# Decoding the weights of a dense layer beside earlier attention units, with four attention units done in split precision instead of plain fp32

## The chip, the cores and the metric

The kernel runs on one core of a Trainium2 chip. The metric is the time of one execution on the device, in microseconds (us). Three runs of the kernel before took 1157.36, 1158.56 and 1164.47 us; their median is 1158.56 us. The engines are named as in the profile: PE is TensorE (matrix products), DVE is VectorE, ACT is ScalarE, POOL is GpSimd, SP is SyncE, which here only issues transfers.

## The reference

Three layers follow one another on 3072 tokens (4 sequences of 768) of width 512. The first is attention with 8 heads of width 64, over a window of 128 positions and 4 sink positions. The second is a dense layer with weights of 512 x 2048 and 2048 x 512 that computes h - tanh(h) between its products. The third is a layer of 8 experts, each with weights of 512 x 1024 and 1024 x 512, of which every token goes through the one that its logits choose.

```python
scores = scale * np.matmul(q, k.transpose(0, 1, 3, 2))
keep = is_sink | in_window
a = softmax(np.where(keep, scores, -1e9))     # written out in the reference
x = np.matmul(a, v)                           # heads side by side: 3072 x 512
h = x @ w_in
x = (h - np.tanh(h)) @ w_out
e_idx = np.argmax(x @ w_gate + modality_bias[modality_id], axis=1)
out[mask] = gate_w[mask, None] * (np.maximum(x[mask] @ w1[e], 0.0) @ w2[e])
```

All of it is in fp32. The kernel reaches that precision in one of two ways: a product of plain fp32 operands, or a product of operands that are split into a high and a low part of type fp32r, of which two or three products are added up in PSUM. The weights w_in and w_out reach the core as 64-bit floats and are turned into 32-bit ones on it.

## The kernel before

**Attention units.** Queries are cut into 12 chunks of 256 tokens; a chunk and a head are a unit, 96 units U in all. `a_load` and `a_loadv` fetch q, k and v of a unit. `a_S` makes two score tiles s (128 queries each): PE computes them, DVE masks them (L317) and takes the row maximum while it copies them to e (L324), ACT exponentiates (L326). `a_norm` divides by the row sum, `a_T` transposes e on PE (L348, L349) into one PSUM tile T, and `a_PV` multiplies by v into the PSUM tile R. The first nf = 14 units are plain: scores are one fp32 product per tile (L315), `a_plain` copies T on ACT, and the product with v is four fp32 products (L406 to L410). All units from 14 on are pair units: `a_split` casts q to A (ACT) and k to K (DVE, L211), and subtracts to get the low parts B (POOL) and the lower half of K (DVE, L214); `a_splitv` does so with v (cast on ACT, subtraction on POOL); scores are two fp32r products (L312, L313); `a_pair` has two more subtractions on DVE (L386 for fl, L387 for sT); the product with v is up to seven fp32r products (L414 to L420), followed by an addition on DVE (L423 for xp). A plain unit's division by the row sum is on ACT (L336), a pair unit's on POOL (L338).

**The dense layer.** It has 16 pairs of weight tiles, f = 0 to 15: `w_load` fetches 128 x 512 64-bit numbers of w_in (rawi) and of w_out (rawo), 512 KB each. `w_decode` turns one such tile into fp32 with three instructions on DVE (L145, L147, L149, by way of a PSUM tile ypi or ypo that shares its two buffers with R), then casts to the high part on ACT (L209) and subtracts for the low part on POOL (L214). For each chunk c and each f, `L1` makes twelve products with w_in (L176) into h, `gact` computes the activation in steps that alternate between ACT and DVE (L187 to L192), `g_split` casts on ACT (L209) and subtracts on POOL (L214), and `L2` makes twelve products with w_out (L246) into acc. `xsplit` (L211 and L214 on xt) splits a chunk's attention output before its `L1`.

**The expert layer.** When eleven chunks are through, routing has sorted their tokens (`r_order`) into pages of 256 tokens of one expert each, and SP reads from the table `order` which expert and which token list each page has. For a page g and f = 0 to 7: `m_wload` fetches 512 KB of weights (mr), `m_wsplit` casts them on ACT (mh, L753) and subtracts on DVE (ml, L754); `m_list` fetches the token list (mpl) and turns it into indices on DVE (mi L764, ms L766), `m_xload` gathers the rows on POOL (mx, L777), `m_xT` transposes them, `m_L1` (L803), `m_L2` (L820) and `m_out` (L829) do the rest. Page 0 begins while the last chunk's dense layer still runs.

**What sets the order.** Every step is added to a list with a number that says when it is due: unit U at 2U - 15.64 plus an offset, `L1` of chunk c and tile f at 16c + f, a page's step at offsets from its own start. The list is sorted by that number and emitted; a scheduler that simulates the engines then decides, instruction by instruction, in which order each engine's queue stands. The numbers are fields of one dictionary in `__init__` (line 45): wl and wls (start and step of the weight loads), wd and wds (of the decodes), nf, and for the pages mwl and mws (how far ahead of its product a page weight is loaded and split). Loads and lists of the first pages are not placed before the number `first`, at which the order of eleven chunks is known. Decoded weights, raw weights and page weights come from one pool of 33 slots, of which 32 hold the decoded weights while the dense layer runs.

Of the kernel before, what the change touches and what calls it, by code (L numbers as in the profile page):

```python
# [40 lines left out]
class Kern:  # L41
    def __init__(self, tc, a):
        self.tc, self.nc, self.a = tc, tc.nc, a
        self.Wi, self.Wo = {}, {}
        self.o = dict(tc='a', xa='g', mt0=-0.28, gz='v', mxe=11, lx='v', nf=14, efh='a', trc=-14.17, tpf=-1.86, xhi='v', vhi='a', vlo='g', qhi='a', khi='v', sT='a', tr='a', ev='a', glo='g', whi='a', wlo='g', gk=0, wl=-8.54, wls=1.25, wd=-3.86, wds=1.05, wo=1, bs=2, be=3, bE=3, bV=1, bg=2, btr=1, bxt=1, pt={'h': 'h', 's': 'r', 'T': 'r', 'R': 'R', 'x': 'R', 'y': 'R'}, pb=(('r', 2), ('h', 2), ('R', 2)), tl=-9.97, ts=-5.86, tv=-4.34, tsv=-2.34, tS=-5.24, dS=0.07, tN=-4, dN=0.5, tT=-1.78, dT=0.35, tPV=-0.39, txs=-0.28, tg=0.64, tre=0.05, trl=0.48, trr=3.39, u0=-15.64, g=2, lag=3.4, raw=2, sp=2, ghi='a', qlo='g', klo='v', eh='v', xlo='v', x2=4, me=13, mxl=8.77, mxt=1.5, mlag=1.45, mwl=9.99, mws=3.27, mm=0, ev0='v', ghi0='a', vhi0='a', sT0='a', qhi0='a', xlo0='g', eh0='v', y=2)

    def e(self, k, start):
        return self.o.get(k + "0", self.o[k]) if start else self.o[k]
# [786 lines left out]
    def m_events(self, add, g, t, t0=-1e9, ts=(0, 1)):  # L835
        n8 = FF // P
        o = self.o
        at = lambda d, fn, *a: add(max(t + d, t0), fn, *a)
        at(-o["me"], self.m_expert, g)
        x0 = o["mxe"] if g == 1 else o["mxl"]  # L840
        if g < EARLY and t0 > 0:
            add(t0, self.m_list, g)
        else:
            at(-x0 - .01, self.m_list, g)
        at(-x0, self.m_xload, g, ts)
        for j in ts:
            at(-o["mxt"] + 0.5 * j, self.m_xT, g, j, ts)
            at(n8 + o["mlag"] - 0.5, self.m_out, g, j)
        for f in range(n8):
            at(f - o["mwl"], self.m_wload, g, f)  # L850
            at(f - o["mws"], self.m_wsplit, g, f)
            at(f, self.m_L1, g, f, ts)
            at(f + o["mlag"], self.m_L2, g, f, ts)

# [205 lines left out]
```

## Time and profile before

| | us |
|---|---|
| median of three runs | 1158.56 |
| profiled execution | 1158.06 |
| its span, from first to last instruction | 1156.3 |
| PE busy in the span | 1109.8 |
| DVE busy | 845.4 |
| ACT busy | 696.1 |
| POOL busy | 586.4 |

The profiled execution's time holds 1.8 us that lie outside the span. The mean clock granted to PE over the span was 0.989 of full speed. Busy times are averages over stages that have different limits: the plain units at the start, the decoding of the weights beside the first chunk, the eleven chunks after it, and the pages. Only what happens in the stage that the change touches says what it is worth. A row of the timeline gives the start in us, the length in us, engine, line, the tile written and the tiles read, how many instructions it groups, and in brackets the idle time before it with what ended it.

### The profile page before, as it was taken

The numbers are of one execution on the slowest core, as the hardware profiler recorded it, in microseconds if no ns is written. First come the engines' busy times: TensorE is split into PE (matmuls) and PEld (weight loads), VectorE is DVE, ScalarE is ACT, GpSimd is POOL, SyncE is SP. The second block draws the span as 40 slices with busy tenths as digits, with TensorE's granted clock in tenths as the row PEclk, the third lists the DMA queues.
The fourth block names the chain that finished last, engine by engine and source line by source line (L and its number), as shares of the span: only waits on it lengthen the run. The fifth ranks groups of instructions, "written<-read, shape, count | busy, mean of one in ns | idle before, by whom it ended". The sixth has DMA issues, their size and how long they took to land. (4 is left out here: it accounts for less than half of the span.)

```text
span 1156.3 us, 22180 instructions
## 1 busy us (share of the span) xinstructions
PE 1109.8 (96%) x7143; PEld 978.2 (85%) x7143; DVE 845.4 (73%) x2244; ACT 696.1 (60%) x1669; POOL 586.4 (51%) x847
## 2 busy tenths in 40 slices
PE   7999889999999999999999999999899999999995
PEld 3467678998999999998999998998788989999984
DVE  3389988787888878798888789765687566666640
ACT  3566656666667666667576666664746555555531
POOL 2257775667676767676676767662203211121111
PEclk9999999999999999999999999999999999999998
DMA  6356422223232322222131322100857776677600
GB/s 201 92 188 220 142 71 49 81 74 69 75 70 70 70 78 62 88 65 86 52 94 52 92 65 68 60 10 19 304 188 247 239 231 219 214 233 239 211 21 22
DMA packets 74957, 136.79 MB, mean 118 GB/s; under 512 B 16144, under 2 KB 51216, under 8 KB 74832
## 3 DMA queue, kind: packets, MB, share of 16 engines
q1 hardware_dynamic: 70064, 122.40, 35.0%
q0 software_dynamic: 4768, 12.87, 3.4%
q8 instruction: 59, 0.97, 0.4%
q14 instruction: 66, 0.54, 0.2%
HBM read 122.60 MB, written 12.91 MB: 117 GB/s over the span
## 5 line engine op out<-in xcount | busy, mean ns | idle before, releaser
L176 PE MATMUL h<-xt,wi 128*128 128x256 f32 x2304 | 349.7, 290 | 10.7 <-ACT wi L209 4.3
L176 PEld LDWEIGHTS h<-xt,wi 128*128 128x128 f32 x2304 | 313.5, 193 | 31.1 <-ACT wi L209 6.1
L246 PE MATMUL acc<-wo,g 128*128 128x512 f32 x1152 | 313.9, 399 | 6.0 <-ACT g L209 5.1
L246 PEld LDWEIGHTS acc<-wo,g 128*128 128x128 f32 x1152 | 201.9, 189 | 39.0 <-ACT g L209 5.7
L754 DVE TENSOR_TENSOR ml<-mr,mh 128x1024 fp32r<-128x1024 f32 x104 | 129.3, 1247 | 57.9 <-ACT mh L753 56.7
L214 POOL TENSOR_TENSOR g<-gy,g 128x512 fp32r<-128x512 f32 x96 | 130.9, 1364 | 74.0 <-ACT g L209 70.1
L803 PE MATMUL mh<-mxt,mh 128*128 128x256 f32 (+1 forms) x832 | 154.4, 282 | 1.0 <-ACT mxt L791 0.7
L803 PEld LDWEIGHTS mh<-mxt,mh 128*128 128x128 f32 x832 | 135.7, 191 | 9.5 <-ACT mxt L791 0.9
L820 PE MATMUL macc<-mh,mg 128*128 128x512 f32 x400 | 141.6, 399 | 0.2
L753 ACT CAST mh<-mr 128x1024 fp32r<-128x1024 f32 x104 | 108.9, 1051 | 44.5 <-PE macc L820 29.6
L356 POOL TENSOR_SCALAR_AFFINE_SELECT X<-fl 128x512 fp32r<-128x512 f32 (+1 forms) x192 | 113.2, 612 | 41.8 <-DVE fl L386 23.5
L829 POOL DMA_INDIRECT out_dram<-mo,mi x25 | 26.2, 1046 | 205.7 <-ACT mo L828 202.0
L326 ACT ACTIVATE e<-e,nm 128x160 f32<-128x160 f32 x192 | 81.7, 426 | 79.9 <-DVE nm L324 71.2
L803 PE MATMUL mh<-mxt,ml 128*128 128x256 f32 (+1 forms) x416 | 117.0, 282 | 0.0
L191 ACT ACTIVATE u<-u,kt 128x512 f32<-128x512 f32 x96 | 69.4, 723 | 45.8 <-DVE h L190 30.8
L324 DVE CUSTOM_DVE_ANT_0 e<-s,mask 128x160 f32<-128x160 f32 x192 | 61.3, 319 | 37.0 <-PE T L349 28.4
L214 DVE TENSOR_TENSOR K<-k,K 64x448 fp32r<-64x448 f32 x82 | 85.3, 1040 | 2.7
L214 POOL TENSOR_TENSOR B<-q,A 128x256 fp32r<-128x256 f32 x82 | 70.6, 861 | 31.5 <-ACT A L209 31.2
L820 PEld LDWEIGHTS macc<-mh,mg 128*128 128x128 f32 x400 | 74.4, 189 | 13.3 <-DVE mg L807 1.0
L806 ACT ACTIVATE mg<-mh 128x256 fp32r<-128x256 f32 (+1 forms) x104 | 39.2, 377 | 75.1 <-PE mh L803 70.6
L187 ACT ACTIVATE u<-h 128x512 f32<-128x512 f32 x96 | 56.4, 588 | 40.0 <-PE h L176 39.7
L803 PEld LDWEIGHTS mh<-mxt,ml 128*128 128x128 f32 x416 | 79.3, 191 | 0.0
(230 smaller groups left out, 2196.1 us busy)
## 6 DMA issues: line engine op xcount, KB each, us to landing
mr<-in_moe_w_dram SPq DMA_DIRECT2D x104, 512.0 KB, 4.7
k<-in_k_dram SPq DMA_DIRECT2D x82, 224.0 KB, 2.6
v<-in_v_dram SPq DMA_DIRECT2D x96, 128.0 KB, 2.4
q<-in_q_dram SPq DMA_DIRECT2D x82, 128.0 KB, 2.3
rawi<-in_moe_w_in_dram SPq DMA_DIRECT2D x16, 512.0 KB, 6.2
rawo<-in_moe_w_out_dram SPq DMA_DIRECT2D x16, 512.0 KB, 5.4
x2d<-x SPq DMA_DIRECT2D x24, 256.0 KB, 2.1
k<-in_k_dram SPq DMA_DIRECT2D x14, 112.0 KB, 2.6
```

The costliest lines, as they stand in the source:

```text
L176: nc.tensor.matmul(h, w[:, wl, k * P:(k + 1) * P], x[:, xl, k], start=(n == 0), stop=(n == 11))
L187: nc.scalar.activation(u, h, AF.Square)
L191: nc.scalar.activation(u, u, AF.Relu, bias=self.kt, accum_out=self.over[:, n:n + 1])
L214: (self.nc.vector if eng == "v" else self.nc.gpsimd).tensor_tensor(out=out, in0=a, in1=b, op=ALU.subtract)
L246: nc.tensor.matmul(o, g[:, gl, q:q + P], w[:, wl], start=(f == 0 and n == 0), stop=(f == NF - 1 and n == 2))
L324: nc.vector.tensor_tensor_reduce(out=e, in0=s[:, P:QW], in1=self.mask[min(i, 2)], scale=-0.125, scalar=3.0e38, op0=ALU.add, op1=ALU.min, a ...
L326: nc.scalar.activation(e, e, AF.Exp, bias=nm, scale=-1.0, accum_out=u["sm"][:, t:t + 1])
L356: self.nc.gpsimd.affine_select(out=out, in_=in_, pattern=[[0, n], [s, P]], base=0, channel_multiplier=-s, compare_op=ALU.is_gt if prev els ...
L753: nc.scalar.copy(hi, r)
L754: nc.vector.tensor_sub(lo, r, f32(hi))
L803: nc.tensor.matmul(h, wt[:, k * P:(k + 1) * P], x[:, xl, k, c0:c0 + w], start=(n == 0), stop=(n == 11))
L820: nc.tensor.matmul(self.macc[g][t], gt[:, gl, i * P:(i + 1) * P], w[:, DM:], start=(f == 0 and n == 0), stop=(f == n8 - 1 and n == 2))
```

## The change

The option dictionary changes in seven numbers, and a page's load and split get numbers of their own for page 0 (mwl0, mws0). The first 10 units are plain instead of 14, so units 10 to 13 become pair units. Weight loads start at -21.0 in steps of 1.9 instead of -8.54 in steps of 1.25, decodes at -14.0 in steps of 1.8 instead of -3.86 in steps of 1.05. A step of 2 is one attention unit. The part of the dictionary that stays is cut here.

```diff
-nf=14, ... wl=-8.54, wls=1.25, wd=-3.86, wds=1.05, ...
+nf=10, ... wl=-21.0, wls=1.9, wd=-14.0, wds=1.8, ...
-mwl=9.99, mws=3.27, ...
+mwl=9.99, mwl0=14.0, mws0=7.0, mws=3.27, ...
         for f in range(n8):
-            at(f - o["mwl"], self.m_wload, g, f)
-            at(f - o["mws"], self.m_wsplit, g, f)
+            at(f - (o["mwl0"] if g == 0 else o["mwl"]), self.m_wload, g, f)
+            at(f - (o["mws0"] if g == 0 else o["mws"]), self.m_wsplit, g, f)
```

SP's queue near the start, kernel before: loads of q, k and v of the units 3 to 6, then the first weight tiles. A number behind a name is the tile's own and tells only tiles of one name apart.

```order
L280 DMA v_230<-in_v_dram 128x256
L262 DMA q_233<-in_q_dram 64x256
L263 DMA k_234<-in_k_dram 64x448
L280 DMA v_272<-in_v_dram 128x256
L262 DMA q_275<-in_q_dram 64x256
L263 DMA k_276<-in_k_dram 64x448
L500 DMA wg<-in_moe_w_gate_dram 128x32
L503 DMA mb<-in_moe_modality_bias_dram 128x16
L506 DMA ids<-in_moe_modality_id_dram 128x24x2
L262 DMA q_365<-in_q_dram 64x256
L263 DMA k_366<-in_k_dram 64x448
L135 DMA rawi_481<-in_moe_w_in_dram 128x1024
L135 DMA rawo_496<-in_moe_w_out_dram 128x1024
L280 DMA v_404<-in_v_dram 128x256
L135 DMA rawi_501<-in_moe_w_in_dram 128x1024
```

SP's queue near the start, the changed kernel: from the load of k of unit 2 on.

```order
L263 DMA k_187<-in_k_dram 64x448
L135 DMA rawi_190<-in_moe_w_in_dram 128x1024
L135 DMA rawo_208<-in_moe_w_out_dram 128x1024
L280 DMA v_210<-in_v_dram 128x256
L262 DMA q_213<-in_q_dram 64x256
L263 DMA k_214<-in_k_dram 64x448
L135 DMA rawi_218<-in_moe_w_in_dram 128x1024
L135 DMA rawo_236<-in_moe_w_out_dram 128x1024
L280 DMA v_238<-in_v_dram 128x256
L262 DMA q_241<-in_q_dram 64x256
L263 DMA k_242<-in_k_dram 64x448
```

A pair of weight tiles, 1 MB, now stands behind the loads of each of the units 2 to 5; before, the first pair stood behind unit 6.

DVE's queue around unit 3, kernel before: its maxima (L324), its mask (L317) and the reciprocal of its sum (L330), then unit 4's first.

```order
L330 RECIPROCAL sm_252<-sm_252 128x2
L324 ISA e_0_296,nm_0_295<-s_0_292,mask_107 128x160
L324 ISA nm_0_295 128x1
L317 COPY_PREDICATED s_1_299<-mgt,s_1_299 128x128
L324 ISA e_1_303,nm_1_302<-s_1_299,mask_118 128x160
L324 ISA nm_1_302 128x1
L211 CAST xt_736<-xp_0_267 128x256
L330 RECIPROCAL sm_294<-sm_294 128x2
L324 ISA e_0_386,nm_0_385<-s_0_382,mask_107 128x160
L324 ISA nm_0_385 128x1
```

DVE's queue around unit 3, the changed kernel, from the reciprocal of unit 2 on; s and e of unit 3 are s_0_306, s_1_313, e_0_310 and e_1_317.

```order
L330 RECIPROCAL sm_262<-sm_262 128x2
L145 TENSOR_SCALAR ypi_379<-rawi_190 128x512
L324 ISA e_0_310,nm_0_309<-s_0_306,mask_107 128x160
L324 ISA nm_0_309 128x1
L147 SCALAR_TENSOR_TENSOR ypi_379<-rawi_190,ypi_379 128x512
L317 COPY_PREDICATED s_1_313<-mgt,s_1_313 128x128
L149 SCALAR_TENSOR_TENSOR yi_378<-rawi_190,ypi_379 128x512
L145 TENSOR_SCALAR ypo_409<-rawo_208 128x512
L147 SCALAR_TENSOR_TENSOR ypo_409<-rawo_208,ypo_409 128x512
L324 ISA e_1_317,nm_1_316<-s_1_313,mask_118 128x160
L324 ISA nm_1_316 128x1
L149 SCALAR_TENSOR_TENSOR yo_408<-rawo_208,ypo_409 128x512
```

The six decode instructions of the first weight pair stand between the rows of unit 3; later units up to 9 have about one pair each between theirs.

SP's queue at page 0, kernel before: the page's first weight tile mr_0, then the token lists of the pages 1 and 2 with the table reads that they need, then the further weight tiles.

```order
L745 DMA mr_0_11532<-in_moe_w_dram 128x1024
L759 TENSOR_LOAD order
L759 ISA x2
L762 ISA
L762 DMA mpl_11543<-xs 128x2x2
L759 TENSOR_LOAD order
L759 ISA x2
L762 ISA
L762 DMA mpl_11558<-xs 128x2x2
L745 ISA
L745 DMA mr_1_11570<-in_moe_w_dram 128x1024
L745 ISA
L745 DMA mr_2_11604<-in_moe_w_dram 128x1024
```

SP's queue at page 0, the changed kernel.

```order
L745 DMA mr_0_11600<-in_moe_w_dram 128x1024
L745 ISA
L745 DMA mr_1_11602<-in_moe_w_dram 128x1024
L745 ISA
L745 DMA mr_2_11604<-in_moe_w_dram 128x1024
L745 ISA
L745 DMA mr_3_11606<-in_moe_w_dram 128x1024
L745 ISA
L745 DMA mr_4_11608<-in_moe_w_dram 128x1024
L759 TENSOR_LOAD order
L759 ISA x2
L762 ISA
L762 DMA mpl_11619<-xs 128x2x2
```

Four more weight tiles now stand ahead of the two lists. On DVE the conversions of these two lists (L764, L766) stood ahead of the activation row L190 of pair 5 of the last chunk and now stand behind that of pair 6; on ACT the cast of the page's first weight tile (L753) stood behind the cast of that chunk's g of pair 5 and now stands ahead of it.

## Rows read from the trace of the kernel before

**Rows 1.** The page: span, busy time of each engine (section 1).

```profile
span 1156.3 us, 22180 instructions
...
PE 1109.8 (96%) x7143; PEld 978.2 (85%) x7143; DVE 845.4 (73%) x2244; ACT 696.1 (60%) x1669; POOL 586.4 (51%) x847
...
```

**Rows 2.** Windows: stretch, length, busy us of PE PEld DVE ACT POOL, PEclk, DMA share, GB/s.

```profile
...
20.00:40.00 20.00, 19.72 (x48) 8.72 (x47) 3.95 (x21) 8.49 (x31) 3.97 (x11) 1.00 0.58 197
40.00:62.00 22.00, 21.81 (x57) 11.09 (x56) 10.52 (x32) 10.11 (x31) 7.07 (x13) 1.00 0.37 104
62.00:163.00 101.00, 86.72 (x461) 67.53 (x460) 95.42 (x209) 64.50 (x163) 74.11 (x90) 0.95 0.49 165
...
20.00:30.00 10.00, 9.91 (x26) 4.41 (x24) 1.68 (x9) 3.65 (x14) 1.56 (x4) 1.00 1.00 347
...
```

**Rows 3.** Waits of DVE, 0 to 62 us: total us, times, longest.

```profile
...
DVE e L324 <- PE T L349: 17.0, 8, 2.9
...
```

**Rows 4.** Timeline of DVE, 46 to 52 us: the first weight decode.

```profile
...
48.47 0.69 DVE L145 TENSOR_SCALAR ypi<-rawi 128x512 int32<-128x512 int32 x1
...
```

**Rows 5.** Timeline of PE, 19 to 30 us: start, length, engine, line, tile.

```profile
...
20.51 1.11 PE L406 MATMUL R<-sTn,v 32*64 32x256 f32 x2
...
24.23 2.39 PE L315 MATMUL s<-k,q 64*128 64x288 f32 x4
26.55 1.11 PE L406 MATMUL R<-sTn,v 32*64 32x256 f32 x2
...
```

**Rows 6.** Groups of DVE by form, 48 to 150 us: busy us, mean ns, idle before.

```profile
...
L147 DVE SCALAR_TENSOR_TENSOR ypi<-rawi,ypi 128x512 int32<-128x512 int32 x16 | 11.0, 688 | 0.0
...
L214 DVE TENSOR_TENSOR K<-k,K 64x448 fp32r<-64x448 f32 x7 | 7.9, 1130 | 0.2
...
L211 DVE CAST K<-k 128x448 fp32r<-128x448 f32 x7 | 5.0, 709 | 0.0
...
L386 DVE TENSOR_TENSOR fl<-T,fl 128x256 fp32r<-128x256 f32 x3 | 1.3, 422 | 0.0
...
```

**Rows 7.** Timeline of DVE, 119 to 163 us: two subtractions for K.

```profile
...
119.30 1.68 DVE L214 TENSOR_TENSOR K<-k,K 64x448 fp32r<-64x448 f32 x1
...
162.32 0.62 DVE L214 TENSOR_TENSOR K<-k,K 64x448 fp32r<-64x448 f32 x1
...
```

**Rows 8.** Timeline of PE, 68 to 76 and 142 to 148 us: plain unit, pair unit.

```profile
...
72.46 0.75 PE L315 MATMUL s<-k,q 64*128 64x288 f32 x2
73.14 0.64 PE L406 MATMUL R<-sTn,v 32*64 32x256 f32 x2
...
74.72 1.20 PE L246 MATMUL acc<-wo,g 128*128 128x512 f32 x4
...
143.43 0.28 PE L414 MATMUL R<-sT,V 128*128 128x256 f32 x1
...
144.18 0.35 PE L312 MATMUL s<-K,A 128*128 128x288 f32 x1
...
144.50 1.99 PE L246 MATMUL acc<-wo,g 128*128 128x512 f32 x8
...
```

**Rows 9.** Waits of PE, 54 to 170 us: total us, times, longest.

```profile
...
PE h L176 <- ACT wi L209: 4.3, 6, 1.3
PE h L176 <- POOL wi L214: 2.4, 4, 0.9
...
```

**Rows 10.** Timeline of ACT, 819 to 832 us: casts before page 0.

```profile
...
823.35 1.06 ACT L753 CAST mh<-mr 128x1024 fp32r<-128x1024 f32 x1 [0.40 <-DMA mr<-in_moe_w_dram]
...
826.02 1.05 ACT L753 CAST mh<-mr 128x1024 fp32r<-128x1024 f32 x1 [1.12 <-DMA mr<-in_moe_w_dram]
...
```

**Rows 11.** Timeline of DVE, 815 to 820 us: the first list row ahead of L190.

```profile
...
817.61 0.17 DVE L764 CAST mi<-mpl 128x2 int32<-128x2 f32 x1 [4.05 <-DMA mpl<-xs]
...
```

**Rows 12.** Timeline of PE, 823 to 836 us: the wait ahead of page 0.

```profile
...
830.85 1.40 PE L246 MATMUL acc<-wo,g 128*128 128x512 f32 x4 [3.93 <-ACT g L209]
832.73 3.18 PE L246 MATMUL acc<-wo,g 128*128 128x512 f32 x8 [0.48 <-POOL g L214]
...
```

More of the change, by code (lines that the diff above doesn't have):

```diff
@@ L44, in __init__ @@
         self.Wi, self.Wo = {}, {}
-        self.o = dict(tc='a', xa='g', mt0=-0.28, gz='v', mxe=11, lx='v', nf=14, efh='a', trc=-14.17, tpf=-1.86, xhi='v', vhi='a', vlo='g', qhi='a', khi='v', sT='a', tr='a', ev='a', glo='g', whi='a', wlo='g', gk=0, wl=-8.54, wls=1.25, wd=-3.86, wds=1.05, wo=1, bs=2, be=3, bE=3, bV=1, bg=2, btr=1, bxt=1, pt={'h': 'h', 's': 'r', 'T': 'r', 'R': 'R', 'x': 'R', 'y': 'R'}, pb=(('r', 2), ('h', 2), ('R', 2)), tl=-9.97, ts=-5.86, tv=-4.34, tsv=-2.34, tS=-5.24, dS=0.07, tN=-4, dN=0.5, tT=-1.78, dT=0.35, tPV=-0.39, txs=-0.28, tg=0.64, tre=0.05, trl=0.48, trr=3.39, u0=-15.64, g=2, lag=3.4, raw=2, sp=2, ghi='a', qlo='g', klo='v', eh='v', xlo='v', x2=4, me=13, mxl=8.77, mxt=1.5, mlag=1.45, mwl=9.99, mws=3.27, mm=0, ev0='v', ghi0='a', vhi0='a', sT0='a', qhi0='a', xlo0='g', eh0='v', y=2)
+        self.o = dict(tc='a', xa='g', mt0=-0.28, gz='v', mxe=11, lx='v', nf=10, efh='a', trc=-14.17, tpf=-1.86, xhi='v', vhi='a', vlo='g', qhi='a', khi='v', sT='a', tr='a', ev='a', glo='g', whi='a', wlo='g', gk=0, wl=-21.0, wls=1.9, wd=-14.0, wds=1.8, wo=1, bs=2, be=3, bE=3, bV=1, bg=2, btr=1, bxt=1, pt={'h': 'h', 's': 'r', 'T': 'r', 'R': 'R', 'x': 'R', 'y': 'R'}, pb=(('r', 2), ('h', 2), ('R', 2)), tl=-9.97, ts=-5.86, tv=-4.34, tsv=-2.34, tS=-5.24, dS=0.07, tN=-4, dN=0.5, tT=-1.78, dT=0.35, tPV=-0.39, txs=-0.28, tg=0.64, tre=0.05, trl=0.48, trr=3.39, u0=-15.64, g=2, lag=3.4, raw=2, sp=2, ghi='a', qlo='g', klo='v', eh='v', xlo='v', x2=4, me=13, mxl=8.77, mxt=1.5, mlag=1.45, mwl=9.99, mwl0=14.0, mws0=7.0, mws=3.27, mm=0, ev0='v', ghi0='a', vhi0='a', sT0='a', qhi0='a', xlo0='g', eh0='v', y=2)
     def e(self, k, start):
```

## The prediction

> **What bounds the kernel now.** I read the page first, then windows by stage, then the waits of the engine that each stage waits for. On the page PE is busy 96% of a span of 1156.3 us and DVE 73% [rows 1]. That is a mean, and it hides where PE stands still. The windows show it [rows 2]: from 20 to 62 us PE is busy 41.5 of 42 us and DVE only 14.5; from 62 to 163 us PE has just 86.7 of 101 us and DVE 95.4. So the first stage, where plain attention runs alone, leaves DVE idle for 27.5 us, and the next, where DVE decodes weights beside chunk 0, is bound by DVE. DVE's idle time in the first is mostly waiting for PE's transposes, 17.0 us [rows 3]; its first decode starts at 48.47 us [rows 4]. What PE waits for in the second are decoded weights: 4.3 us on ACT's and 2.4 us on POOL's part of wi [rows 9], both of which follow DVE's.
>
> The plain stage also runs PE slowly: one unit takes 26.55 - 20.51 = 6.04 us [rows 5]. Four score products take 2.39 us there, while two take 0.75 us at 72.46 us [rows 5, 8]. The clock column prints 1.00 for both, so I trust the durations: the plain stage is at the lower level (1.2 GHz), the later rows are at 2.4 GHz.
>
> A second hole lies ahead of page 0: PE waits 3.93 us for a cast of g on ACT and 0.48 us on POOL, and the eight products after it take 3.18 us [rows 12] against 1.99 us for the same eight at the higher level [rows 8].
>
> **Decodes and their loads, moved.** A pair is six DVE instructions of about 0.69 us [rows 4, 6], 4.1 us; 16 pairs are 96 instructions. In the trace 11 are done by 62 us, which leaves 85. In the changed queue 48 stand ahead of unit 10's scores. Do they fit? DVE was busy 3.95 us in 20 us of plain units [rows 2], that is 1.2 us a unit; with 4.1 us for a pair it is 5.3 of 6.04 us, so they do, tightly. The scores at 24.23 us are unit 4's, so unit 10's would come 6 x 6.04 us later, at 60.5; the new order puts 18 products of chunk 0 ahead of or beside them. Eight products of 512 columns take 1.99 us [rows 8], so one of 256 takes about 0.12 us, 0.25 at the lower level: 4.5 us, which is work that would have come later anyway. PE is at unit 10's scores at about 65 us. So the DVE-bound stretch begins with 85 - 48 = 37 decode instructions fewer, 37 x 0.69 = 25.5 us.
>
> The loads go along: one pair is 1 MB, a plain unit's q, k and v are 64 + 112 + 128 = 304 KB. 1.3 MB per 6.04 us are 217 GB/s; from 20 to 30 us the same queues moved 347 GB/s while PE was busy 9.91 of 10 us [rows 2]. That cover hides them. If it were gone, each of the four pairs now ahead of units 3 to 6 would make a unit late by 1 MB at 347 GB/s, 2.9 us, 11.6 us in all. Behind them on SP stand only the next units' loads, which are issued more than a unit early. I take nothing.
>
> **Four units in pairs.** At equal clock a plain unit's scores take 2 x 0.68 us (72.46 to 73.14 for one half), its product with v 1.58 us (73.14 to 74.72); a pair unit's take 2 x 0.32 us (144.18 to 144.50) and 0.75 us (143.43 to 144.18) [rows 8]. The transposes are the same. PE saves 2.94 - 1.39 = 1.55 us a unit, 6.2 us. DVE pays: K cast 0.71, K subtraction 1.13, fl 0.42 and the like for sT and xp [rows 6], 3.1 us a unit, 12.4 us. POOL takes over two subtractions and the division by the row sum, but loses the low parts of six pairs that are made earlier; it was busy 74.1 of 101 us [rows 2] and stays third.
>
> The K subtraction varies from 0.62 to 1.68 us [rows 7], and its mean of 1.13 us is what I use. The Trainium skill, SBUF — State Buffer, section "SBUF: two separate sides", speaks against the change: a DVE instruction with two inputs in SBUF and a GpSimd one exclude each other on a shared port pair, and the loser waits for the whole instruction. If by that rule all four new subtractions ran at the longest row, 4 x (1.68 - 1.13) = 2.2 us would be added, and the forecast would be 1142. No row here shows who waits for whom; the spread is all that the trace has.
>
> **The sum of the early stage.** DVE in the stretch: 95.4 - 25.5 + 12.4 = 82.3 us. With its idle time of 5.6 us kept that is 87.9 instead of 101 us: 13.1 us gained. PE, if it waited for nothing, would need 86.7 - 6.2 = 80.5 us: 20.5 us gained at most. At the other end nothing is gained, if DVE's decodes in the plain stage make PE wait there for what they save later. I take 15 us, near DVE's bound, since DVE still has the most to do, and somewhat above it, because a part of its idle time was waiting for plain units that are pair units now.
>
> **Page 0.** Four weight tiles pass two token lists on SP. Before, ACT waited 0.40 and 1.12 us for tiles that were issued behind the lists [rows 10]; and DVE stood 4.05 us at the first list's conversion, with L190 of the last chunk, hence its g, queued behind it [rows 11]. Both waits go. But ACT now must cast the page's first tile, which is not issued earlier, ahead of g, so of DVE's 4 us I let about 1 arrive. 1.5 + 1 = 2.5 us of PE's 3.93 us; and with a shorter standstill the eight products stay at the higher level, 3.18 - 1.99 = 1.2 us. About 3.5 us. Bounds: 0, if ACT's new order costs what it saves, and 3.9 + 0.5 + 1.2 = 5.6 us. The two lists come later by four issues; their rows are wanted only a page later, some 40 us on. Nothing.
>
> **Sum.** 1158.06 (the profiled execution, 1156.3 of it span) - 15 - 3.5 = 1139.6, so **1140 us**, 1.6% under the median of 1158.56, from which the profiled run differs by 0.5.
>
> **Rivals.**
>
> *B, three engines in turn.* Each weight passes DVE, ACT, POOL. After unit 10 all three have about the same amount left, and the waits for wi of 6.7 us [rows 9] come back in full although the first eight pairs are ready. Then the early gain is 15 - 6.7 = 8.3, the page's 1.5 if ACT pays for the new cast's place: 1148. For it speaks the long chain, against it that eight pairs are then in hand.
>
> *C, the decodes only trade places.* DVE's queue is in order, so a maximum (L324) behind a decode may be late by one instruction, 0.69 us, or two; eight units at 1.5 us lose 12 us of the 15. Then about 1155. For it: the order puts all six decodes between rows of one unit, and only 0.7 us of a unit's 6.04 is left. Against it: PE is a unit ahead in scores, with two buffers.
>
> *D, the clock rises earlier.* PE was 98% busy from 20 to 62 us with plain products and stayed at the lower level [rows 2, 5]; the higher one shows at 72 us, after products of the dense layer began. The 18 such products that are now placed earlier could bring it forward by some 12 to 14 us, of which half is won, 6 to 7: 1133. By the Trainium skill, TensorE: Matmul & The Clock Gate, section "What's actually happening", throttling is the default state and activity releases it. The busy plain stage at the lower level does not bear that out for this kind of activity; the 18 products are another kind.
>
> *E, slower: the lower level lasts.* PE stands still more often while it waits for weights after unit 10, and falls to 1.2 GHz. Each us of work there costs one more. With 18.5 us gained, it decides once 18.5 us of work more run at the lower level. Half of the stretch, 40 us, would give 1158 - 18.5 + 40 = 1180. Against it: the stretch as it is has a granted clock of 0.95 [rows 2], 5 us lost, with more idle time than I expect.
>
> **How the numbers follow.** Chances: forecast 0.62 (its own range 1134 to 1146), B 0.16, C 0.08, D 0.09, E 0.05. About 1% is what a measurement of this kernel tells from no change, that is 1147 to 1170 us. Faster by over 1%: forecast, D and half of B, 0.79. Within 1%: the rest of B, and C, 0.16. Slower: E, 0.05. The range leaves out C, E and the edge of D and B: **1131 to 1150**; upward it takes in B, downward D's middle and the larger bounds (20.5 and 5.6 would give 1132).
>
> **What would show it.** Right: decodes from about 26 us on in DVE's timeline, plain units still 6.04 us, unit 10's scores near 65 us, the end of chunk 0's second product some 15 us earlier than 167 us, DVE near 82 us of work from unit 10 to there, PE's wait ahead of page 0 under 2 us. Wrong: plain units over 6.5 us (C); the waits for wi at 6 us or more (B); score products of plain units at 0.35 us apiece before 64 us (D); eight L246 products at over 3 us in the middle of the stretch (E); PE waiting for k or v in the first 40 us (the loads).

## The result and the profile after

The changed kernel takes 1148.2 us, the median of four runs (1144.07 to 1149.33), against 1158.87 us for the kernel before, the median of four runs of which three are those named at the start. The ratio is 0.9891 with a 95% interval of 0.9856 to 0.9926. That is 10.7 us, or by the ratio some 12.6 us, where the prediction had 18.5 (1140 us, range 1131 to 1150). The profiled execution took 1148.85 us, with a span of 1147.1 us.

To see where the time came from I follow two events through both traces: ACT's first copy of acc after chunk 10 (x<-acc), and the output rows (mo, L828). A row is start, length, engine, line, tiles, and the idle time before it; the row of L828 groups all 25 and gives their shortest, median and longest length in ns and the first and the last start. Before:

```profile
...
784.81 1.28 ACT L209 COPY x<-acc 128x512 f32<-128x512 f32 x2 [2.88 <-PE acc L246]
...
L828 ACT ACTIVATE mo<-macc,mpl x25: 676/687/715, 869.9 to 1142.8; 128x512 f32<-128x512 f32 x25
...
```

After:

```profile
...
777.50 1.27 ACT L209 COPY x<-acc 128x512 f32<-128x512 f32 x2 [2.88 <-PE acc L246]
...
L828 ACT ACTIVATE mo<-macc,mpl x25: 677/687/710, 861.4 to 1133.8; 128x512 f32<-128x512 f32 x25
...
```

Chunk 10 ends 784.81 - 777.50 = 7.3 us earlier; the first output row, page 0's, is written 8.5 us earlier (861.4 against 869.9), the last 9.0 us (1133.8 against 1142.8). So the profiled pair puts 7.3 us on the early stage, where 15 were predicted, and 1.7 us on all that follows, where 3.5 were.

**The early stage as a balance of DVE.** Two stretches that differ by this lead of 7.3 us are 0 to 163 us before and 0 to 155.7 us after. Windows, before (columns as in [rows 2]; the stretch 62 to 163 stands there):

```profile
...
0.00:62.00 62.00, 54.98 (x131) 26.51 (x132) 24.24 (x117) 26.20 (x84) 16.29 (x56) 1.00 0.49 142
...
```

After:

```profile
...
0.00:62.00 62.00, 53.98 (x131) 27.11 (x131) 44.48 (x144) 30.63 (x90) 28.86 (x64) 1.00 0.80 231
62.00:155.70 93.70, 83.63 (x452) 69.41 (x452) 84.76 (x193) 57.55 (x149) 70.16 (x92) 0.91 0.39 124
...
```

DVE's third number is what counts. Before, it worked 24.24 + 95.42 = 119.7 of 163 us and was idle for 43.3. After, it worked 44.48 + 84.76 = 129.2 of 155.7 us and was idle for 26.5. It has 9.6 us more to do and 16.9 us less of idle time: 16.9 - 9.6 = 7.3 us, the whole lead. The idle time was won in the plain stage (37.8 us before, 17.5 after); behind it, it grew from 5.6 to 8.9.

That the three numbers close is arithmetic, since the stretches were chosen to differ by 7.3 us; what the balance adds is where the idle time lies. The two stretches do not end at one point of the work either. Chunk 0's result leaves the dense layer (x<-acc on DVE) 10.45 us earlier, where the prediction had named some 15. Before, then after:

```profile
...
167.13 0.67 DVE L211 COPY x<-acc 128x512 f32<-128x512 f32 x1
...
```

```profile
...
156.68 0.68 DVE L211 COPY x<-acc 128x512 f32<-128x512 f32 x1
...
```

Attention lags meanwhile: unit 16's first scores come at 128.84 us, 2.5 us later than before (126.31). Only from the end of chunk 4 on is the lead about 7.1 us (402.80 against 409.90) and nearly constant up to chunk 10.

The waits of PE from 62 to 170 us answer to [rows 9]:

```profile
...
PE s L312 <- DVE nm L324: 3.2, 5, 1.1
PE h L176 <- DVE xt L214: 1.6, 2, 1.4
PE s L312 <- DVE sT L387: 1.3, 2, 0.7
PE T L348 <- POOL e L338: 1.1, 1, 1.1
PE h L176 <- POOL wi L214: 0.9, 2, 0.6
PE h L176 <- ACT wi L209: 0.9, 2, 0.5
...
```

The waits for wi fell from 6.7 to 1.8 us. What PE waits for now is DVE's part of the attention units: their maxima (nm), the low part of the transposes (sT) and the split of chunk 1's input (xt).

### The profile page after: what moved, and what is told of

Read it like the earlier page. It is cut to its first block, busy times and chain, and to the rows that moved or that the text cites. A ratio compares the mean times of both kernels' runs of the same rounds, so it can differ in the third digit from the quotient of the medians.

```text
span 1147.1 us, 22235 instructions
## 1 busy us (share of the span) xinstructions
PE 1105.3 (96%) x7139; PEld 980.2 (85%) x7139; DVE 856.4 (75%) x2264; ACT 697.3 (61%) x1669; POOL 607.6 (53%) x863
## 5 line engine op out<-in xcount | busy, mean ns | idle before, releaser
L214 POOL TENSOR_TENSOR g<-gy,g 128x512 fp32r<-128x512 f32 x96 | 133.5, 1391 | 61.7 <-ACT g L209 59.2
L753 ACT CAST mh<-mr 128x1024 fp32r<-128x1024 f32 x104 | 108.6, 1051 | 43.7 <-PE macc L820 27.8
L214 DVE TENSOR_TENSOR K<-k,K 64x448 fp32r<-64x448 f32 x86 | 97.7, 1136 | 2.9
L214 POOL TENSOR_TENSOR B<-q,A 128x256 fp32r<-128x256 f32 x86 | 73.8, 858 | 40.0 <-ACT A L209 39.0
L214 POOL TENSOR_TENSOR V<-v,V 128x256 fp32r<-128x256 f32 x86 | 68.6, 797 | 25.3 <-ACT V L209 25.1
L324 DVE CUSTOM_DVE_ANT_0 e<-s,mask 128x160 f32<-128x160 f32 x192 | 61.1, 318 | 24.1 <-PE T L349 16.6
```

The source lines that it names most:

```text
L214: (self.nc.vector if eng == "v" else self.nc.gpsimd).tensor_tensor(out=out, in0=a, in1=b, op=ALU.subtract)
L324: nc.vector.tensor_tensor_reduce(out=e, in0=s[:, P:QW], in1=self.mask[min(i, 2)], scale=-0.125, scalar=3.0e38, op0=ALU.add, op1=ALU.min, a ...
L753: nc.scalar.copy(hi, r)
```

## Experiments

Kernels of one group ran on one chip and are compared with the kernel before on that chip, whose median was between 1156 and 1161 us there; so ratios are compared, not times.

### The parts one by one

One kernel has the page's two numbers alone, one the early loads and decodes alone, one the 10 plain units alone, and one the last two together:

```diff
 e1_page_only:     mwl0=14.0, mws0=7.0                       (else as before)
 e2_weights_only:  wl=-21.0, wls=1.9, wd=-14.0, wds=1.8      (else as before)
 e3_units_only:    nf=10                                     (else as before)
 e4_no_page:       nf=10 and the four of e2                  (else as before)
```

> Before with the page 0 numbers alone (mwl0 = 14, mws0 = 7); 14 plain units, weights as before. My theory from the two traces: page 0 gives 1.7 us (a lead of 7.3 us at the last chunk grows to 9.0 at the later pages), because the clock stays up there but PE's waits only change their place: about 1157. If the 3.5 us of the prediction were right and something else ate them, 1155.

> Before with the early loads and decodes alone; 14 plain units, page as before. Theory 1 (DVE's sum from the first pair unit on decides): DVE is 25 us of decodes ahead and has no new pair units to pay for, so PE is the bound, and the four units stay plain; 5 to 9 us faster than before, 1150 to 1154. Rival (the two parts only work together, since the plain units' PSUM and DVE slots hold the gain): within 2 us of before.

> Before with 10 plain units alone; weights and page as before. Theory 1 (DVE bound): DVE has 12.4 us more to do in the stretch that it bounds, and starts on it earlier by less than that: 3 to 8 us slower than before, 1162 to 1167. Rival (PE bound, the 6.2 us of PE that pair units save show): 1152.

> The changed kernel with page 0 as before: early weights and 10 plain units. Both theories: the lead of 7.3 us that the trace shows at the last chunk, so about 1151. If parts add up, e4 and e1 together give the changed kernel's 10.7 us; if the page's gain depends on the early stage, they don't.

| kernel | median, us (before: 1160.75) | ratio | 95% interval |
|---|---|---|---|
| page alone | 1158.27 | 0.9979 | 0.9954 to 1.0004 |
| weights alone | 1146.48 | 0.9883 | 0.9824 to 0.9942 |
| units alone | 1173.33 | 1.0105 | 1.0073 to 1.0137 |
| weights and units | 1147.64 | 0.9894 | 0.9838 to 0.9950 |

The early decodes carry the change. Alone they gave 14 us, more than the 5 to 9 that I expected. The four pair units alone cost 12.6 us, more than the 3 to 8 expected, although by the prediction's sum they save PE 6 us. With the early decodes they give and take nothing that these intervals can show. The page's part is at most 5.3 us, by its interval, and its median of 2.5 us is not clear of nothing; the two medians with and without it (1148.2 and 1147.64, on two chips) show none of it. Nor do the four profiles of this group: from the copy of acc after chunk 10 to the end of the span, page alone takes 370.0 us, weights alone 370.0, units alone 370.7, weights and units 369.7. The 1.7 us of the first pair of profiles (371.5 against 369.6) are not seen again here.

Units alone, 62 to 163 us, and the waits of PE for wi from 50 to 165 us:

```profile
...
62.00:163.00 101.00, 81.59 (x404) 68.39 (x402) 93.50 (x210) 58.96 (x150) 76.29 (x94) 0.83 0.47 156
...
```

```profile
...
PE h L176 <- ACT wi L209: 7.0, 7, 1.9
PE h L176 <- POOL wi L214: 4.8, 5, 1.5
...
```

PE has less to do and waits longer: 11.8 us for wi instead of 6.7 [rows 9], with DVE busy 93.5 of 101 us. That fits the reading that work moved to DVE, where DVE is the bound, costs its full length there: 12.4 us were worked out for four units, 12.6 measured. But the granted clock fell too, to 0.83 from 0.95 [rows 2], and in this profile chunk 10 ends at 802.78 us, 18.0 us later than in the profile of before; so that the two figures nearly agree is in part luck.

Weights alone, up to 151.5 us:

```profile
...
0.00:62.00 62.00, 52.04 (x134) 26.04 (x134) 45.86 (x150) 31.17 (x93) 29.88 (x67) 0.87 0.80 232
62.00:151.50 89.50, 82.52 (x447) 64.00 (x447) 69.31 (x166) 55.10 (x147) 57.88 (x74) 0.92 0.39 123
...
```

Chunk 10 ends at 773.35 us in this profile, 11.5 us before 784.81, and the stretch is cut accordingly. DVE works 45.86 + 69.31 = 115.2 us, 14 us less than in the changed kernel, and yet chunk 10 ends only 4.2 us earlier than there, of which a clock that rose at 39 us in this profile may have given some 2 (last section). Here PE, with four more plain units and 7 us of idle time behind 62 us instead of 10, is nearer to the bound.

### Taking work off DVE, and fewer or more plain units

```diff
 e5_k_cast_act:    khi0='a'   (after; k's high part of units 10 to 15 on ACT)
 e6_k_low_pool:    klo0='g'   (after; k's low part of units 10 to 15 on POOL)
 e8_twelve_plain:  nf=12      (after)
 e9_plain14_all:   nf=14      (after)
```

> The changed kernel with the high part of k (the cast L211 for K) of units 10 to 15 on ACT instead of DVE. If DVE still bounds the stretch from the first pair unit to the end of chunk 0, it loses six casts of about 0.7 us, 4 us, and the time falls by 2 to 4 us against the changed kernel (ratio to before 0.986 to 0.988). If PE's clock and the chain of the weights decide, nothing changes (0.989).

> The changed kernel with the low part of k (the subtraction L214 for K) of units 10 to 15 on POOL instead of DVE. In the changed kernel's trace eleven such subtractions take 11.8 us on DVE, and each is 0.62 us long plus what is left of a POOL subtraction that was running when it began. If that wait and DVE's sum decide, DVE loses 6 to 7 us and the time falls by 4 to 6 us (ratio 0.984 to 0.986). If POOL, which gets six more subtractions ahead of the weights' low parts, becomes the bound, the time rises by 2 us or more.

> The changed kernel with 12 plain units instead of 10. Weights alone and 14 plain units gave 0.988, 10 plain units without the page 0.989. If the number of plain units only trades PE's gain for DVE's loss, 12 lie between or a little below both: 0.986 to 0.989. If pair units are worth their 1.55 us each on PE, 12 are slower than 10 by 3 us: 0.992.

> The changed kernel with 14 plain units as before: early weights and the page's numbers. If the four pair units gave nothing, this is as fast as the changed kernel or faster: 0.985 to 0.989. If they gave the 6.2 us of PE's time that the prediction counted, it is slower than the changed kernel by 3 us or more: 0.992.

| kernel | median, us (before: 1159.23) | ratio | 95% interval |
|---|---|---|---|
| k cast on ACT | 1140.93 | 0.9856 | 0.9812 to 0.9900 |
| k low part on POOL | 1143.34 | 0.9874 | 0.9832 to 0.9915 |
| 12 plain units | 1142.86 | 0.9866 | 0.9829 to 0.9903 |
| 14 plain units | 1144.26 | 0.9875 | 0.9835 to 0.9915 |

All four lie below the changed kernel's 0.9891, by 0.0016 to 0.0035, and all four intervals overlap with its own. What can be said: with early decodes, 14 plain units are faster than the changed kernel's 10 by 0.0016, give or take 0.0053. If the four pair units were worth their 1.55 us each, 14 would be slower by 6.2 us, 0.0053, which lies outside; so they are not worth that. The cast on ACT shows 4 us against the changed kernel, by the ratios, as DVE's bound says, and the larger relief, the subtraction on POOL, 2 us where 4 to 6 were expected; but both are known to some 6 us only. The kernel with the cast on ACT has the lowest time of all that were run, 1140.93 us, and by its interval it is faster than the kernel before; that it beats the changed kernel is likely and not shown.

### Both reliefs together, and the page's splits

```diff
 e7_split_late:     mws0=3.27                        (after)
 e10_twelve_k_act:  nf=12, khi0='a'                  (after)
 e11_twelve_k_off:  nf=12, khi0='a', klo0='g'        (after)
```

> The changed kernel with page 0's splits due as before (mws0 = 3.27), its loads still early. On ACT the cast of the page's first tile is then behind the cast of g of pair 5 of the last chunk again. If that cast ahead of g is what brought PE's wait of 1.47 us on POOL's g there, the wait goes and the waits ahead of page 0 fall from 4.1 to about 2.6 us; the lead at page 0's first output row grows by about 1 us. If the gathers and transfers set it, nothing changes.

> The changed kernel with 12 plain units and the high part of k of units 12 to 15 on ACT. Each alone gave 0.9866 and 0.9856. If both relieve DVE in the same stretch and PE's clock is the next limit, together they give 0.984 to 0.986; if they add up, 0.982 to 0.983.

> As the one with 12 plain units and the cast on ACT, and with the low part of k on POOL too, so that DVE has nothing to do for k in units 12 to 15. If DVE is still the bound: another 2 to 3 us, 0.982 to 0.984. If POOL's chain of weights or PE's clock is: no faster than 12 plain units alone, 0.986 or above.

The one with 12 plain units and the cast on ACT took 1149.32 us against 1161.25, ratio 0.9900 (0.9867 to 0.9933); with the subtraction on POOL as well 1151.6 us, 0.9917 (0.9893 to 0.9941). The first is slower than either expectation, the second is as its rival said: relieving DVE further gave nothing. Not all of the first one's distance from 12 plain units alone lies in the early stage: from the copy of acc after chunk 10 to the end of the span it takes 372.1 us, the other, on another chip, 368.0. The second has DVE at 79.65 of 101 us and is still no faster:

```profile
...
62.00:163.00 101.00, 90.95 (x491) 74.25 (x491) 79.65 (x190) 64.36 (x170) 74.05 (x98) 0.92 0.37 121
...
```

```profile
...
PE s L312 <- DVE sT L387: 3.5, 3, 2.2
PE T L348 <- DVE nm L324: 2.8, 2, 2.1
...
```

PE waits 3.5 and 2.8 us for DVE here with DVE idle for a fifth of the time. That speaks against DVE's sum as what decides here, and for the order in which three engines hand a unit on: scores, maximum, exponential, transposes, low parts, product, each in a queue that is served in order. No run shows it.

Page 0 with its splits at their old place (one run, 1148.14 us) left its waits from 790 to 845 us at

```profile
...
PE acc L246 <- ACT g L209: 2.1, 1, 2.1
PE acc L246 <- POOL g L214: 1.5, 2, 1.2
```

3.6 us instead of 4.1 in the changed kernel (its rows stand further below), not the 2.6 that I expected: the waits for POOL's g shrank, and a wait for ACT's came back. As far as one run can tell, the position of that one cast is not what holds page 0.

### Chunk 0 held back

```diff
         t = self.xt[c]
+        if c == 0 and pr < 3:
+            self.cast("v", t[:, 0, pr], self.xp[0, 3])
         self.cast(self.e("xhi", c == 0), t[:, 0, pr], xp)
```

> The changed kernel with chunk 0's input held back until the last of its four parts is there (three casts more on DVE, 1.2 us, which write values that the real casts overwrite), so that none of the 18 products of chunk 0 stands among the plain units. Unit 10's scores then come at 61 to 63 us instead of 67.3. Theory 1 (the stretch from there to the end of chunk 0 lasts as long as DVE's sum, whenever it starts): the lead over before grows from 7.3 to 9 to 12 us, ratio 0.985 to 0.988. Theory 2 (the 18 products only change places, and they are what lifts PE's clock during the plain units in some executions): no higher clock before unit 10 in the trace, and no faster than the changed kernel, 0.989 to 0.992.

The three casts let the scheduler place other steps anew too: from 25 to 32 us on, the queues of all engines differ from the changed kernel's. It took 1144.54 us against 1156.33, ratio 0.9896 (0.9873 to 0.9919). Timeline of PE and the window 62 to 163 us (its line numbers are higher by two: L317 is the plain scores, L314 the pair scores):

```profile
...
55.49 2.40 PE L317 MATMUL s<-k,q 64*128 64x288 f32 x4
...
62.93 0.61 PE L314 MATMUL s<-K,A 128*128 128x288 f32 x1 [1.48 <-DVE nm L326]
...
```

```profile
...
62.00:163.00 101.00, 90.40 (x546) 79.95 (x547) 95.28 (x215) 63.68 (x164) 77.76 (x104) 0.93 0.37 115
...
```

The rows are as expected: unit 10's scores come at 62.93 instead of 67.32 us, and no plain scores run above the lower level before that (2.40 us for four). By the ratio the kernel is no faster than the changed one, as theory 2 said, though part of theory 1's range lies inside the interval. Its trace is nearer to theory 1, which had a lead of 9 to 12 us:

```profile
...
772.58 1.28 ACT L211 COPY x<-acc 128x512 f32<-128x512 f32 x2 [2.88 <-PE acc L248]
...
```

Chunk 10 ends 4.9 us earlier than in the changed kernel's profile (777.50, on another chip), 12.2 us earlier than before. So the 4.4 us by which the stretch starts earlier are kept in this profile. That the median does not show them may be because the clock's early rise, which some executions of the changed kernel's early stage had (last section), is lost here; no run separates the two.

## Why the prediction was right, and where it was wrong

**The direction and its cause were right.** Decodes in the plain stage are what gained: alone they give 0.9883, some 13.6 us, as much as all three parts together within the intervals. The first decode starts even earlier than the 26 us I named:

```profile
...
18.91 0.67 DVE L145 TENSOR_SCALAR ypi<-rawi 128x512 int32<-128x512 int32 x1
...
```

Loads are hidden, as said; up to 65 us PE waits for k only at the very start (5.7 us before), in one place for a maximum, and 0.4 us for ACT:

```profile
...
PE s L315 <- DMA k<-in_k_dram: 5.6, 1, 5.6
PE s L315 <- DVE nm L324: 1.3, 1, 1.3
...
```

**The step that failed is the sum of the early stage**, in two terms and one bound. 15 us were forecast, 7.3 came. The first term is the stretch's start. I took 25.5 us off a DVE stretch that begins at 62 us in both kernels, and had written ahead of the sum that the changed one begins at about 65. Before, unit 10's scores stand at

```profile
...
62.75 2.28 PE L315 MATMUL s<-k,q 64*128 64x288 f32 x4
...
```

In the changed kernel's trace they stand at 67.32 (PE; plain scores of units 4, 5, 6, then unit 10):

```profile
...
24.08 2.40 PE L315 MATMUL s<-k,q 64*128 64x288 f32 x4
...
32.59 2.28 PE L315 MATMUL s<-k,q 64*128 64x288 f32 x4 [1.33 <-DVE nm L324]
...
39.54 2.29 PE L315 MATMUL s<-k,q 64*128 64x288 f32 x4
...
67.32 0.61 PE L312 MATMUL s<-K,A 128*128 128x288 f32 x1 [0.55 <-DVE nm L324]
...
```

From unit 4 to unit 10 it is 67.32 - 24.08 = 43.24 us, where six units at 6.04 us are 36.24. Of the 7.0 us more, unit 5's scores waited 1.33 us for a maximum that stood behind a decode on DVE, which is rival C's mechanism, once, and unit 10's 0.55 us; the other 5.1 us are the 18 products, for which 4.5 had been worked out. So four of these six units took over 6.5 us, the sign named for C, mostly because of the products. From 67.3 us on, the stretch lasts 155.7 - 67.3 = 88.4 us, and the sum had said 87.9. So 13.1 us become 13.1 - 5.3 - 0.5 = 7.3. That 88.4 and 87.9 lie so near is luck in part, as they are made up otherwise:

```profile
...
67.30:155.70 88.40, 78.86 (x439) 67.32 (x440) 79.63 (x180) 54.76 (x141) 67.36 (x87) 0.90 0.38 118
...
```

DVE works 79.6 us there and is idle for 8.8, where the sum had 82.3 and 5.6. In the balance of DVE above, the later start shows as idle time in the plain stage: 25.5 us of decodes were to fill it, and it shrank by 20.3. The second term is the 1.9 us that I added to DVE's bound because a part of its idle time was waiting for plain units. That idle time did not go: behind 62 us it grew from 5.6 to 8.9 us. The bound is PE's 6.2 us for pair units, which stood in the upper end of the range: the runs show no such worth.

**Rival B had the time, 1148, and not the mechanism.** It let the waits for wi come back at 6.7 us; they are 1.8. That the early gain was about half gone was right, but by the later start and by waits for attention's own steps on DVE. The measured time lies nearer to B's number than to the forecast, and in the range because the range took B in.

**Rival E in small.** The window 62 to 155.7 us has a granted clock of 0.91, against 0.95 before: (1 - 0.91) x 93.7 = 8.4 us lost instead of 5.1. PE's standstills of 0.3 to 1.4 us while it waits for DVE are spread over 110 to 150 us there, and the lower level returns three times.

**Page 0 was over-sized.** PE's waits from 790 to 845 us are now

```profile
...
PE acc L246 <- POOL g L214: 2.8, 2, 1.5
PE mh L803 <- DVE gy L192: 0.8, 1, 0.8
PE acc L246 <- ACT g L209: 0.5, 1, 0.5
```

4.1 us in all, where they were 4.4 [rows 12] and were to be under 2. The one long standstill became four short ones. Timeline of PE, with the waits in brackets:

```profile
...
812.18 2.12 PE L246 MATMUL acc<-wo,g 128*128 128x512 f32 x8 [1.47 <-POOL g L214]
...
821.38 1.20 PE L246 MATMUL acc<-wo,g 128*128 128x512 f32 x4 [0.47 <-ACT g L209]
823.94 2.10 PE L246 MATMUL acc<-wo,g 128*128 128x512 f32 x8 [1.36 <-POOL g L214]
...
```

The 3.93 us on ACT's g went down to 0.47, more than the 2.5 I gave it, and with no long standstill the clock stayed up: the eight products at 823.94 take 2.10 us instead of 3.18, which is 1.1 of the 1.7 us that did arrive. That is not sure to happen: of the eight other kernels that have both of the page's numbers, five show a granted clock of 0.87 to 0.94 from 815 to 842 us. But the next link of the chain was late each time. Timeline of POOL:

```profile
...
808.57 1.00 POOL L777 DMA_INDIRECT mx<-x2d,ms  x1 [6.48 <-ACT gy L188]
809.87 0.96 POOL L777 DMA_INDIRECT mx<-x2d,ms  x1 [0.31 <-issue]
810.85 1.28 POOL L214 TENSOR_TENSOR g<-gy,g 128x512 fp32r<-128x512 f32 x1
...
821.04 1.41 POOL L777 DMA_INDIRECT mx<-x2d,ms  x1 [0.30 <-issue]
822.47 1.42 POOL L214 TENSOR_TENSOR g<-gy,g 128x512 fp32r<-128x512 f32 x1
...
```

The gathers of page 1 (821.04), which I had costed at nothing because their rows are wanted a page later, now stand ahead of POOL's part of the next g, which begins as they end (822.47), and PE waits 1.36 us for it. The gathers of page 0 (808.57, 809.87) had done the same to the g before (810.85), for 1.47 us; they wait for the first token list. (The bracket names ACT's gy, but the gather starts 0.43 us after DVE begins to write its indices ms at 808.14, as it does before the change.) DVE converts the list at

```profile
...
808.06 0.17 DVE L764 CAST mi<-mpl 128x2 int32<-128x2 f32 x1 [3.41 <-DMA mpl<-xs]
...
```

The list was issued at 804.51 us in SP's timeline, 3.55 us before that row; before the change it was issued at 811.48 and converted at 813.34, 1.86 us later. Weight tiles were issued right behind it in both. That the four more of them slow it is not borne out: the other kernels with the same order on SP have 1.9 to 2.9 us, and those without it 1.9 to 2.9 as well. What made it late stays open. The question for a moved step is not only who needs its result, but who stands behind it in its queue.

**What stays open.** Whether the changed kernel gains 10.7 or 12.6 us, and which of the variants from 0.9856 to 0.9900 is best: their intervals are 0.002 to 0.006 wide to each side, and a median of four runs depends on how many of them had the early rise of the clock (below). Why two reliefs of DVE together are no better than one is argued from the waits above and not shown by a run of its own; a part of the distance may be the clock: four plain scores at 39 us took 1.23 us in the profile of the kernel with 12 plain units and 2.29 in that of the one with the cast on ACT as well.

## What to carry to other kernels

An engine that is idle in one stage and the bound of the next is worth filling early; count the gain as the idle time that it will really lose, from the first to the last instruction of both stages, not as work taken out of the second stage. Where one engine is the bound, work moved to it from another can cost more than the other saves: four units cost 12.6 us alone, for 6.2 us of the other engine's time by the prediction's sum. For every step that is moved, look at what stands behind it in the queue of each engine that it uses.

## What the runs showed of the hardware

**A subtraction on DVE waits for one on POOL to end.** The low part of k, two operands in SBUF, takes 0.62 us alone and up to 1.70. DVE and POOL in the changed kernel:

```profile
...
106.74 1.70 DVE L214 TENSOR_TENSOR K<-k,K 64x448 fp32r<-64x448 f32 x1
...
145.52 0.62 DVE L214 TENSOR_TENSOR K<-k,K 64x448 fp32r<-64x448 f32 x1
...
```

```profile
...
106.67 1.29 POOL L214 TENSOR_TENSOR wo<-yo,wo 128x512 fp32r<-128x512 f32 x1
107.92 1.12 POOL L214 TENSOR_TENSOR V<-v,V 128x256 fp32r<-128x256 f32 x1
...
118.28 0.74 POOL L214 TENSOR_TENSOR V<-v,V 128x256 fp32r<-128x256 f32 x1 [0.61 <-ACT V L209]
...
```

At 106.74 DVE's subtraction begins 0.07 us behind one of POOL's that ends at 107.96; 0.48 us later, at 108.44, DVE's ends. At 145.52 none runs on POOL, and it takes 0.62. All long ones of both traces up to 160 us have this form: nine after and six before end 0.47 to 0.49 us behind the POOL instruction that was running, mostly a subtraction. The next POOL subtraction, which asks for 0.74 us elsewhere (118.28), takes 1.12 when it starts while DVE's is running (107.92). The Trainium skill, SBUF — State Buffer, section "SBUF: two separate sides", says of the port pair that the two engines share that a DVE instruction with two inputs in SBUF, or a GpSimd one, whichever starts first, keeps it for its whole length while the other is blocked. The trace agrees, in both directions. In the changed kernel eleven such subtractions took 11.8 us up to 156 us, instead of 6.8; the prediction's mean of 1.13 us held that price already (1.07 measured).

**The clock can rise inside the plain stage, in some executions.** The changed kernel and the one without the page have the same instructions in the same order up to 790 us. The plain scores at 39.5 us took 2.29 us in the one profile (above) and 1.47 in the other:

```profile
...
39.55 1.47 PE L315 MATMUL s<-k,q 64*128 64x288 f32 x4
40.95 0.64 PE L406 MATMUL R<-sTn,v 32*64 32x256 f32 x2
...
```

PE went to the higher level there for some 7 us, shortly after products of the dense layer had run among the plain ones, and fell back after waits of 0.9 us at 44 and 46 us. That execution ended chunk 10 at

```profile
...
775.15 1.27 ACT L209 COPY x<-acc 128x512 f32<-128x512 f32 x2 [2.87 <-PE acc L246]
...
```

2.35 us before the other, 2.07 of which it had at unit 10's scores already (65.25 against 67.32). The kernel with the late splits of page 0, a third execution of the same instructions up to page 0, has the rise at 61 us and ended chunk 10 at 776.40. With the products held back, the profile shows no such rise before unit 10.

The mean granted clock of an execution hints at which kind it was. The profile prints 1.00 until the clock's first change, although scores of 2.4 us are at the lower level, so an early rise that is lost again lowers the printed mean: 0.974 to 0.979 in the six profiles of kernels with early decodes that show it, 0.984 to 0.994 in the five others. In eight of the nine such kernels with four runs or more and products among the plain units, every run with a mean of 0.982 or less is shorter than every one with 0.983 or more; in the ninth, the changed kernel, one of its three (1149.33 us, at 0.974) is longer than the 1148.85 us at 0.988. The means of the two kinds differ by 1.3 to 4.1 us. All four runs with the products held back have 0.985 to 0.989. So rival D exists, but not in every execution, and it is worth some 1 to 4 us, not 6 to 7. It is a part of the spread of the runs; the spread of the changed kernel, 1144 to 1149 us, it explains only in part.
